# Attention kernel: VectorE's gather, statistics and root in parts over several steps, the transposed maxima copied by VectorE, the projected sum ahead of a pair of maxima

## The chip, the core and the metric

The kernel runs on one core of one Trainium2 chip. A core has a matrix engine (TensorE, PE in the profile, with its weight loads listed apart as PEld), VectorE (DVE), ScalarE (ACT), GpSimd (POOL) and SyncE (SP, which here only issues transfers). Each engine takes its own instructions strictly in the order in which they were written, and waits on semaphores that other engines or transfers raise. The metric is the device time of one execution in microseconds (us); smaller is better. Inputs and outputs are float32.

## What is computed

Two layers are computed twice in alternation, each added to its input. Layer A is a Fourier mixing of normalised rows, layer B is attention with 32 query heads that share one key head and one value head of width 16:

```python
def _layernorm(x, axis=-1, eps=1e-5): ...   # (x - mean) / sqrt(var + eps)
def _A_ref(x, ...):      # x: (1, 2048, 512)
    a = einsum("bsd,ed->bse", x, dft_hid_re); b = einsum("bsd,ed->bse", x, dft_hid_im)
    return einsum("ts,bse->bte", dft_seq_re, a) - einsum("ts,bse->bte", dft_seq_im, b)
def _B_ref(x, wq, wk, wv, wo):   # 32 heads of 16
    q = heads(x @ wq); k = x @ wk; v = x @ wv
    p = softmax(einsum("bhqd,bkd->bhqk", q, k) * 16 ** -0.5)
    return merge(einsum("bhqk,bkd->bhqd", p, v)) @ wo
x = x + _A_ref(_layernorm(x)); x = x + _B_ref(_layernorm(x))
x = x + _A_ref(_layernorm(x)); x = x + _B_ref(_layernorm(x))
```

## The kernel before

The program is one long instruction list, written by Python loops. Nothing reorders it afterwards: the place in the loops at which a call stands is the place of its instructions in each engine's queue. `make_layer` builds one pair of layers A and B, and it is called twice (L = 0 and L = 1). Each pair has two stages.

`phase_a` is the Fourier mixing, and towards its end the queries, keys and values. It also computes some of the maxima of the scores early. At its very end it gathers the maxima of the first half of row tile 0 (`max_neg`), issues twelve further maxima, and after the third of them `max_rows`.

`phase_b` is the attention. The 2048 query rows are 16 row tiles (i), and each row tile has 32 steps (s_): two halves of the heads times 16 blocks of 128 keys. In one step TensorE computes

- the value products of two steps earlier (`pv`, line 787: eight matrix instructions into the bank z),
- four score products (`score`, line 773) into two pairs of banks named x, which ScalarE turns into exponentials with two instructions (line 776),
- about three products for maxima of later row tiles (`max_half`, line 350) into one of three banks named y, which VectorE reduces to one maximum each (line 351).

The bank y is a pool of three, shared by everything else that is small: the output projection `po`, and the transposed maxima. A bank is used again when its reader has finished, so a matrix product into a y bank waits on the VectorE or ScalarE instruction that read the earlier content.

The softmax needs the maximum of each row before its scores. When all maxima of a row tile are there, `max_neg` (at step 27 of the row tile before) reduces the partial maxima to their negative (`nm`, line 366), rounds it into `ms` (372) and takes the rest of the rounding beside it (373). Two steps later `max_rows` transposes `ms` on TensorE into a y bank (379), copies it to SBUF as `mt` (381) and sends it by four transfers into two extra rows of the transposed queries `qT` (386), so that the score product subtracts the maximum by itself.

The output of a row tile is finished during the next row tile by `out_tasks`, a table from step to calls. At step 12 `o_proj` runs twelve projection products (`o_mm`, lines 86 to 88) into the y bank `po`, with two maxima after the sixth and two after the twelfth (`more_max`), and then `o_add` adds `po` to the residual row in SBUF (`bt["x"]`, line 852) and stores it. In L = 0, where the result is the input of the next layer A, its normalisation follows: `o_stats` at step 14 (statistics by lines 135 and 136), `o_rstd` at step 16 (the inverse root: lines 157, 165 and 166 on VectorE, then three rounds of four small instructions on GpSimd), and the rest on GpSimd at steps 25 to 27. In L = 1 (`last`) these three do nothing. For the last two row tiles no maxima are left, so `o_proj` has its pairs of maxima within row tiles 1 to 14 of each layer.

Of the kernel before, what the change touches and what calls it, by code (L numbers as in the profile page):

```python
# [8 lines left out]
F32 = mybir.dt.float32  # L9
F32R = mybir.dt.float32r  # L10
I32 = mybir.dt.int32
AF = mybir.ActivationFunctionType
ALU = mybir.AluOpType
# [4 lines left out]
P = 128  # L18
# [5 lines left out]
NK = D // P  # L24
TB = 4
NPAIR = H // 2
EPS = 1e-5
# [15 lines left out]
HALF = NPAIR // 2  # L43
# [3 lines left out]
def fnet_mqa_kernel(ctx: ExitStack, tc: tile.TileContext, x_in, ct, dt_, wq, wkv, wo, out):  # L47
# [105 lines left out]
    def ln_rstd(t0, n, table=True, between=lambda: None):  # L153
        v = sb.tile([P, 4], F32, name="lnv", bufs=2)[:, :n]
        w = sb.tile([P, 4], F32, name="lnw", bufs=2)[:, :n]
        r = rs[:, t0:t0 + n]
        nc.vector.tensor_scalar(v, mv[:, t0:t0 + n, 1], EPS, None, op0=ALU.add)
        if table:
            nc.scalar.activation(w, v, AF.Sqrt)
            between()  # L160
            nc.vector.reciprocal(r, w)
            between()
            rounds = 1
        else:
            nc.vector.tensor_scalar(w.bitcast(I32), v.bitcast(I32), 1, None, op0=ALU.logical_shift_right)
            nc.vector.tensor_scalar(r.bitcast(I32), w.bitcast(I32), -1, 0x5F3759DF, op0=ALU.mult, op1=ALU.add)
            rounds = 3
        e = nc.vector if table else nc.gpsimd
        for _ in range(rounds):
            if n == 1 and table:  # L170
                e.scalar_tensor_tensor(w, r, v, r, op0=ALU.mult, op1=ALU.mult)
            else:
                e.tensor_mul(w, r, r)
                e.tensor_mul(w, w, v)
            between()
            e.tensor_scalar(w, w, -0.5, 1.5, op0=ALU.mult, op1=ALU.add)
            between()
            e.tensor_mul(r, r, w)
            between()

    def ln_apply(dst, x, t, eng=None):
        (eng or nc.vector).tensor_scalar(dst, x, mv[:, t, 0:1], rs[:, t:t + 1], op0=ALU.subtract, op1=ALU.mult)
# [4 lines left out]
    def make_layer(L, src, mid, dst, last):  # L187
# [173 lines left out]
            if k is None:  # L361
                o.loaded.add(i)

        def max_neg(i, p0=0, n=NPAIR, k=4):
            nm = sb.tile([P, NPAIR, 2], F32, name="nm")[:, :n, :]
            nc.vector.tensor_reduce(nm, o.mxp[i][:, p0:p0 + n, :, :k], op=ALU.max, axis=AX.X, negate=True)
            if p0 + n == NPAIR:
                o.mxp.pop(i)
            nmv = nm.rearrange("p a g -> p g a")
            ms = sb.tile([P, 2, 2, NPAIR], F32, name="ms").rearrange("p g r a -> p (g r a)")  # L370
            ms = ms[:, :4 * n].rearrange("p (g r a) -> p g r a", g=2, r=2)
            nc.vector.tensor_copy(ms[:, :, 0, :].bitcast(F32R), nmv)
            nc.vector.tensor_sub(ms[:, :, 1, :].bitcast(F32R), nmv, ms[:, :, 0, :])
            st["ms"] = ms

        def max_rows(i, p0=0, n=NPAIR, queue=None):
            queue = queue or nc.sync
            pt = bank("y")[:4 * n, :P]
            nc.tensor.transpose(pt, st["ms"].rearrange("p a b c -> p (a b c)"), ident)
            mt = sb.tile([64, P], F32R, name="mt")[:4 * n, :]  # L380
            nc.scalar.copy(mt, pt)  # L381
            for g in range(2):
                for r in range(2):
                    row = 64 * g + M0 + r
                    q = queue if r else nc.sync
                    q.dma_start(f(o.qT[i][row:row + 1, p0:p0 + n, :]), f(mt[n * (2 * g + r):n * (2 * g + r + 1), :]))
# [148 lines left out]
        def phase_a(extra):  # L535
# [191 lines left out]
            for g in range(4):  # L727
                q_half(14, g, *xt[1], lambda: take(mb, 1 if g else 0))
                if g == 0:
                    v_tr(12, 4, vt[0])  # L730
            max_neg(0, 0, HALF, 5)
            for k in range(12):
                more_max()
                if k == 2:
# [101 lines left out]
        def o_mm(k):  # L836
            if k == 0:
                bt["po"] = bank("y")
            ks = slice(k * P, (k + 1) * P)
            mm3(bt["po"], bt["oh"][:, ks], bt["ol"][:, ks], woh[:, k, :], wol[:, k, :], k == 0, k == NK - 1)  # L840

        def o_proj(i):
            for k in range(NK):
                o_mm(k)
                if k % 2 and i < NT - 1:
                    for _ in range(2):
                        more_max()
                        o.extra += 1
            o_add(i)

        def o_add(i):
            nc.vector.tensor_add(bt["x"], bt["po"], bt["x"])  # L852
# [27 lines left out]

        o.finish = finish

        def o_stats(i):
            if not last:
                ln_stats(bt["x"], i)

        def o_rstd(i):
            if not last:
                ln_rstd(i, 1, table=False)

        def o_ln(i):
            if not last:
# [15 lines left out]
        def phase_b(nxt):  # L908
# [10 lines left out]
            for n in range(NT * NSTEP):  # L919
                i, s_ = divmod(n, NSTEP)  # L920
                if len(behind) == 2:
                    pv(*behind.pop(0))
                behind.append((i, s_))
                g = units[o.done][2] if o.done < len(units) else 1
                for j, m in ((1 - g, 1), (g, 2), (3 - g, 0), (2 + g, 1)):
                    score(i, s_, j)
                    for _ in range(m):
                        if owed(n) >= 1:
                            more_max()
                if i == 0 and 2 <= s_ <= 8 and s_ % 2 == 0:  # L930
                    q_half_store(14, s_ // 2 - 1)
                if n == 12:
                    osp = slot(3, F32R).rearrange("p (a h n) -> p a h n", a=2, h=2)
                if i == 0 and s_ in (12, 14, 16, 18):
                    j = s_ // 2 - 6
                    split_sb(st["wo", j], woh[:, j, :], wol[:, j, :], nc.gpsimd)
                if i > 0:
                    for fn in out_tasks(i - 1).get(s_, ()):
                        fn()
                if s_ == 2:  # L940
                    for j in range(2, NT):
                        if i == max(0, j - 4 if j < 13 else j - 2):
                            qT_load(j)
                for fn in half_tasks(i).get(s_, ()):
                    fn()
                for at, j, p0, np_ in ((NT - AHEAD, i, HALF, HALF), (NSTEP - AHEAD, i + 1, 0, HALF if i == NT - 2 else NPAIR)):
                    if j in (0, NT - 1) or j == i + 1 < NT:
                        if s_ == at:
                            assert done_with(j, p0 + np_ - 1)
                            max_neg(j, p0, np_)  # L950
                        if s_ == at + 2:
                            max_rows(j, p0, np_)
            if nxt is not None:
# [11 lines left out]
        def out_tasks(i):  # L965
            return {
                1: [lambda: o_store(i, 1), lambda: o_sum(i, 1), lambda: x_load(i)], 5: [lambda: o_inv(i, 1)],
                6: [lambda: o_load(i, 1)], 9: [lambda: o_scale(i, 1)], 10: [lambda: o_hi(i, 1)],
                12: [lambda: o_proj(i)], 14: [lambda: o_stats(i)], 16: [lambda: o_rstd(i)],
                25: [lambda: o_ln(i)], 26: [lambda: o_xnh(i)], 27: [lambda: o_xnl(i)],  # L970
            }

# [49 lines left out]
```

## Time and profile before

| quantity | value |
|---|---|
| median of 3 runs | 3721.35 us (3719.64 to 3724.51) |
| the profiled execution | 3724.12 us, its span 3722.3 us |
| busy in the span: PE, DVE, ACT, POOL | 3631.1, 2798.4, 2400.3, 777.3 us |
| phase_b of L = 0 | about 689 to 1866 us of the span |
| phase_b of L = 1 | about 2540 to 3712 us |
| mean granted TensorE clock | 0.990 |

All times inside the execution are us from the start of the span. Where a row has a bracket, such as [0.24 <-PE y L350], the engine sat idle for that long before the row's first instruction, and what ended the wait is named behind the arrow. Rows of the timeline merge neighbouring instructions of one kind (x3 is three of them, and the second number is the time from the first one's start to the last one's end). Consecutive VectorE instructions overlap a little, so three reductions of 0.68 us take 1.89 us. Busy time of PE is modelled from the starts and says little by itself.

### The profile page before, as it was taken

To read this page: it belongs to the slowest core of one execution; us is meant where nothing else is said; L and a number is where in the kernel's file an instruction comes from. 1 tells how busy PE (TensorE), PEld (TensorE's weight loads), DVE (VectorE), ACT (ScalarE), POOL (GpSimd) and SP (SyncE) were. 2 spreads that over 40 slices of the span, in tenths; PEclk is the share of its full clock that TensorE was granted. 3 is DMA by queue.
4 is the path that set the end of the run, shared out by engine and by line. 5 is a ranking of instruction groups with operands and counts; after the bars stand their busy time and mean duration, and the time that the engine had idled before them with its cause. 6 is when DMAs were issued, how large, how long until landed. Compare 5 with 4: busy or idle time off the path is not lost. (4 is left out here: it accounts for less than half of the span.)

```text
span 3722.3 us, 64512 instructions
## 1 busy us (share of the span) xinstructions
PE 3631.1 (98%) x25474; PEld 1909.3 (51%) x25474; DVE 2798.4 (75%) x4767; ACT 2400.3 (64%) x3104; POOL 777.3 (21%) x984
## 2 busy tenths in 40 slices
PE   8999999999999999999999999999999999999999
PEld 6786768533433333334377766684343334333333
DVE  5167978788888888888311779778888888888882
ACT  4322222688888888888933231227888888888888
POOL 5534332111111111111154342421000000000000
PEclk9999999999999999999999999999999999999999
DMA  5444241311111100110143342313111111001100
GB/s 176 133 136 125 97 119 52 101 32 50 33 36 31 49 22 24 33 47 23 40 131 104 129 124 92 110 64 89 47 33 36 33 49 34 22 22 50 33 24 25
DMA packets 204736, 243.00 MB, mean 65 GB/s; under 512 B 36880, under 2 KB 160784, under 8 KB 197264
## 3 DMA queue, kind: packets, MB, share of 16 engines
q1 hardware_dynamic: 199504, 222.08, 20.1%
q0 software_dynamic: 4864, 16.78, 1.5%
q8 instruction: 199, 3.26, 0.4%
q14 instruction: 105, 0.86, 0.1%
q10 hardware_dynamic: 64, 0.02, 0.0%
HBM read 174.58 MB, written 63.17 MB: 64 GB/s over the span
## 5 line engine op out<-in xcount | busy, mean ns | idle before, releaser
L776 ACT ACTIVATE slot<-x 128x1024 f32<-128x1024 f32 x1990 | 1943.1, 1027 | 334.4 <-PE x L773 265.5
L351 DVE TENSOR_REDUCE mxp<-y 128x1 f32<-128x512 f32 x3040 | 1908.1, 684 | 281.5 <-PE y L350 233.3
L787 PE MATMUL z<-slot,v 128*32 128x512 f32 x8192 | 1096.3, 605 | 1.9 <-ACT row L790 1.9
L773 PE MATMUL x<-slot,kz 64*128 64x512 f32 x2956 | 900.9, 447 | 3.6 <-DMA slot<-mt 3.5
L773 PEld LDWEIGHTS x<-slot,kz 64*128 64x128 f32 x2956 | 375.3, 185 | 731.5 <-ACT slot L776 598.5
L350 PE MATMUL y<-kz,slot 64*128 64x512 f32 x2208 | 726.2, 435 | 4.8 <-ACT mt L381 0.7
L338 DVE TENSOR_REDUCE mxe<-y 128x1 f32<-128x512 f32 x832 | 516.4, 682 | 189.4 <-PE y L336 184.7
L660 PE MATMUL x<-ch,xnh 64*128 64x512 f32 (+1 forms) x2048 | 507.8, 390 | 16.3 <-DVE slot L74 8.9
L660 PE MATMUL x<-ch,xnl 64*128 64x512 f32 (+1 forms) x2048 | 475.2, 369 | 0.0
L660 PE MATMUL x<-cl,xnh 64*128 64x512 f32 (+1 forms) x2048 | 474.7, 369 | 0.0
L350 PEld LDWEIGHTS y<-kz,slot 64*128 64x128 f32 x2208 | 349.5, 185 | 94.5 <-DVE mxp L351 27.5
L827 POOL TENSOR_TENSOR row<-row,row 128x256 f32<-128x256 f32 x63 | 46.3, 735 | 1677.8 <-DMA row<-rd 1422.6
L336 PE MATMUL y<-kz,slot 64*128 64x512 f32 (+1 forms) x1088 | 354.3, 420 | 33.7 <-DVE mxe L338 20.7
L78 POOL TENSOR_TENSOR cl<-craw,ch 128x512 fp32r<-128x512 f32 x236 | 303.1, 1303 | 289.2 <-ACT ch L77 229.3
L787 PEld LDWEIGHTS z<-slot,v 128*32 128x32 f32 x8192 | 163.6, 108 | 277.3 <-issue 249.2
L660 PEld LDWEIGHTS x<-ch,xnh 64*128 64x128 f32 x2048 | 268.7, 189 | 69.2 <-issue 16.4
L660 PEld LDWEIGHTS x<-ch,xnl 64*128 64x128 f32 x2048 | 280.7, 189 | 33.3
L660 PEld LDWEIGHTS x<-cl,xnh 64*128 64x128 f32 x2048 | 281.7, 190 | 28.0
L77 ACT CAST ch<-craw 128x512 fp32r<-128x512 f32 x256 | 154.8, 620 | 161.8 <-PE x L660 89.5
L666 ACT COPY junk<-x 128x2 f32<-128x2 f32 x256 | 40.5, 158 | 332.3 <-PE x L660 253.6
L336 PEld LDWEIGHTS y<-kz,slot 64*128 64x128 f32 x1088 | 171.8, 188 | 129.4 <-DVE mxe L338 90.5
L338 DVE TENSOR_REDUCE mxp<-y 128x1 f32<-128x512 f32 (+1 forms) x256 | 144.4, 617 | 24.7 <-PE y L336 21.5
(148 smaller groups left out, 3141.7 us busy)
## 6 DMA issues: line engine op xcount, KB each, us to landing
craw<-ct_in SPq DMA_DIRECT2D x112, 512.0 KB
slot<-qd SPq DMA_DIRECT2D x44, 1024.0 KB
qd<-row SPq DMA_DIRECT2D x144, 128.0 KB
od<-row SPq DMA_DIRECT2D x252, 64.0 KB
row<-x_in SPq DMA_DIRECT2D x32, 256.0 KB
mid<-row POOLq DMA_DIRECT2D x32, 256.0 KB, 2.4
craw<-ct_in SPq DMA_DIRECT2D x32, 256.0 KB
row<-mid SPq DMA_DIRECT2D x32, 256.0 KB
```

The costliest lines, as they stand in the source:

```text
L77: nc.scalar.copy(hi, raw)
L78: (eng or nc.vector).tensor_sub(lo, raw, f(hi))
L336: nc.tensor.matmul(pm[g], o.qT[i][gs, pr, :], kz[gs, c0:c0 + n], start=True, stop=True)
L338: nc.vector.reduce_max(to[:, g:g + 1], pm[g], axis=AX.X)
L350: nc.tensor.matmul(pm, o.qT[i][gs, pr, :], kz[gs, kb * 512:kb * 512 + 512], start=True, stop=True)
L351: nc.vector.reduce_max(partial(i)[:, pr, g, kb:kb + 1], pm, axis=AX.X)
L660: nc.tensor.matmul(z[d][:, cols], w, hl[j][t == 1][rs_], start=m == 0 and ph == 0 and j == t == 0, stop=j == 1 and t == 2 and (ph == 0 or ...
L666: nc.scalar.copy(junk, zp[dd][:, :, cols.start])
L773: nc.tensor.matmul(st["e"][:, g, :], kz[64 * g:64 * g + KR, c * P:(c + 1) * P], o.qT[i][64 * g:64 * g + KR, cp:cp + 4, :], start=True, sto ...
L776: nc.scalar.activation(ptiles[i, s_][:, 2 * w:2 * w + 2, :], st.pop("e"), AF.Exp, scale=DH ** -0.5)
L787: nc.tensor.matmul(a[32 * j:32 * j + 32, :], v1[:, c, :], pt[:, j, :], start=c == 0, stop=c == NT - 1)
L827: nc.gpsimd.tensor_mul(bt["ot"][:, cs], bt["ot"][:, cs], bt["den"][:, cs])
```

## The change

Four edits. First, `max_neg` is cut in two: the negative maximum is reduced at step 27, and `max_split` does the rounding and its rest at step 28; the call at the end of `phase_a` still does both at once (`whole`). Second, the copy of the transposed maxima to `mt` goes from ScalarE to VectorE, at the same place in the program. Third, `o_add` is called right after the twelfth projection product, ahead of the second pair of maxima. Fourth, the statistics of a finished row are taken in two halves of 256 columns at steps 14 and 15, put together at step 16, and the three VectorE instructions of the inverse root come one by one at steps 17, 18 and 19, with GpSimd's part behind the last of them.

```diff
+    def ln_piece(t, k):
+        r = rs[:, t:t + 1]
...
+        if k == 0:
+            nc.vector.tensor_scalar(v, mv[:, t:t + 1, 1], EPS, None, op0=ALU.add)
+        elif k == 1:
+            nc.vector.tensor_scalar(w.bitcast(I32), v.bitcast(I32), 1, None, op0=ALU.logical_shift_right)
+        elif k == 2:
+            nc.vector.tensor_scalar(r.bitcast(I32), w.bitcast(I32), -1, 0x5F3759DF, op0=ALU.mult, op1=ALU.add)
+        else:
+            for _ in range(3):
...              # the same four GpSimd instructions as in ln_rstd
-        def max_neg(i, p0=0, n=NPAIR, k=4):
+        def max_neg(i, p0=0, n=NPAIR, k=4, whole=False):
             nm = sb.tile([P, NPAIR, 2], F32, name="nm")[:, :n, :]
             nc.vector.tensor_reduce(nm, o.mxp[i][:, p0:p0 + n, :, :k], op=ALU.max, axis=AX.X, negate=True)
...
+            st["nm"] = nm
+            if whole:
+                max_split()
+
+        def max_split():
+            nmv = st.pop("nm").rearrange("p a g -> p g a")
...
             nc.vector.tensor_copy(ms[:, :, 0, :].bitcast(F32R), nmv)
...
             mt = sb.tile([64, P], F32R, name="mt")[:4 * n, :]
-            nc.scalar.copy(mt, pt)
+            nc.vector.tensor_copy(mt, pt)
...
-            max_neg(0, 0, HALF, 5)
+            max_neg(0, 0, HALF, 5, True)
...
         def o_proj(i):
             for k in range(NK):
                 o_mm(k)
+                if k == NK - 1:
+                    o_add(i)
                 if k % 2 and i < NT - 1:
                     for _ in range(2):
                         more_max()
                         o.extra += 1
-            o_add(i)
...
-        def o_stats(i):
+        def o_stats(i, h):
             if not last:
-                ln_stats(bt["x"], i)
-
-        def o_rstd(i):
+                if h == 0:
+                    bt["st"] = sb.tile([P, 2, 6], F32, name="bst2")
+                nc.vector.bn_stats(bt["st"][:, h, :], bt["x"][:, 256 * h:256 * h + 256])
+
+        def o_aggr(i):
             if not last:
-                ln_rstd(i, 1, table=False)
+                nc.vector.bn_aggr(mv[:, i, :], bt["st"].rearrange("p a b -> p (a b)"))
+
+        def o_rstd(i, piece):
+            if not last:
+                ln_piece(i, piece)
...
                             max_neg(j, p0, np_)
+                        if s_ == at + 1:
+                            max_split()
                         if s_ == at + 2:
                             max_rows(j, p0, np_)
...
-                12: [lambda: o_proj(i)], 14: [lambda: o_stats(i)], 16: [lambda: o_rstd(i)],
+                12: [lambda: o_proj(i)], 14: [lambda: o_stats(i, 0)], 15: [lambda: o_stats(i, 1)], 16: [lambda: o_aggr(i)],
+                17: [lambda: o_rstd(i, 0)], 18: [lambda: o_rstd(i, 1)], 19: [lambda: o_rstd(i, 2), lambda: o_rstd(i, 3)],
```

VectorE's queue in L = 0 from the middle of one row tile on, before. `mxp<-y` are the maxima of line 351, `row<-y,row` is the sum of `o_add`, and `bst`, `mv`, `lnv`, `lnw`, `rs` are the statistics and the root:

```order
L351 TENSOR_REDUCE mxp_14018<-y 128x1 x25
L852 TENSOR_TENSOR row_14537<-y,row_14537 128x512
L351 TENSOR_REDUCE mxp_14018<-y 128x1 x6
L135 BN_STATS bst<-row_14537 128x6
L136 BN_AGGR mv<-bst 128x2
L351 TENSOR_REDUCE mxp_14018<-y 128x1 x6
L157 TENSOR_SCALAR lnv<-mv 128x1
L165 TENSOR_SCALAR lnw<-lnv 128x1
L166 TENSOR_SCALAR rs<-lnw 128x1
L351 TENSOR_REDUCE mxp_14018<-y 128x1 x17
```

The same place after (line 372 is line 351 of before, 880 is 852):

```order
L372 TENSOR_REDUCE mxp_14024<-y 128x1 x23
L880 TENSOR_TENSOR row_14544<-y,row_14544 128x512
L372 TENSOR_REDUCE mxp_14024<-y 128x1 x8
L915 BN_STATS bst_14872<-row_14544 128x6
L372 TENSOR_REDUCE mxp_14024<-y 128x1 x3
L915 BN_STATS bst_14872<-row_14544 128x6
L372 TENSOR_REDUCE mxp_14024<-y 128x1 x3
L919 BN_AGGR mv<-bst_14872 128x2
L372 TENSOR_REDUCE mxp_14024<-y 128x1 x3
L190 TENSOR_SCALAR lnv<-mv 128x1
L372 TENSOR_REDUCE mxp_14024<-y 128x1 x3
L192 TENSOR_SCALAR lnw<-lnv 128x1
```

The sum has moved ahead of two maxima (25 and 6 have become 23 and 8), and one statistics or root instruction now stands alone behind the three maxima of each step, instead of two or three together.

VectorE's queue around the gather of the maxima at steps 27 to 29, before:

```order
L351 TENSOR_REDUCE mxp_14018<-y 128x1 x15
L366 TENSOR_REDUCE nm<-mxp_11944 128x32
L372 CAST ms<-nm 128x2x16
L373 TENSOR_TENSOR ms<-nm,ms 128x2x16
L351 TENSOR_REDUCE mxp_14018<-y 128x1 x30
```

And after, where 387 is the line 366 of before, and 399 and 400 are 372 and 373:

```order
L372 TENSOR_REDUCE mxp_15075<-y 128x1 x15
L387 TENSOR_REDUCE nm<-mxp_12993 128x32
L372 TENSOR_REDUCE mxp_15075<-y 128x1 x3
L399 CAST ms<-nm 128x2x16
L400 TENSOR_TENSOR ms<-nm,ms 128x2x16
L372 TENSOR_REDUCE mxp_15075<-y 128x1 x3
L408 CAST mt<-y 64x128
L372 TENSOR_REDUCE mxp_15075<-y 128x1 x24
```

Three maxima have come between the gather and the rounding, and the copy to `mt` has joined VectorE's queue behind three more.

VectorE's queue at the end of `phase_a` of L = 0, after; before, sixteen maxima followed line 373 without a copy among them, and the copy stood in ScalarE's queue:

```order
L387 TENSOR_REDUCE nm<-mxp_2801 128x16
L399 CAST ms<-nm 128x2x8
L400 TENSOR_TENSOR ms<-nm,ms 128x2x8
L372 TENSOR_REDUCE mxp_2801<-y 128x1 x3
L408 CAST mt<-y 32x128
L372 TENSOR_REDUCE mxp_2801<-y 128x1 x13
```

The copy now stands behind the third maximum. On TensorE, SyncE and GpSimd the instructions stand in the order in which they stood, except that GpSimd's part of the root comes three steps later.

More of the change, by code (lines that the diff above doesn't have):

```diff
@@ L179, in ln_rstd @@
             between()
+    part = {}
+    def ln_piece(t, k):
+        r = rs[:, t:t + 1]
+        if k == 0:
+            part["v"] = sb.tile([P, 4], F32, name="lnv", bufs=2)[:, :1]
+            part["w"] = sb.tile([P, 4], F32, name="lnw", bufs=2)[:, :1]
+        v, w = part["v"], part["w"]
+        if k == 0:
+            nc.vector.tensor_scalar(v, mv[:, t:t + 1, 1], EPS, None, op0=ALU.add)
[5 more added lines that the diff above has]
+            for _ in range(3):
+                nc.gpsimd.tensor_mul(w, r, r)
+                nc.gpsimd.tensor_mul(w, w, v)
+                nc.gpsimd.tensor_scalar(w, w, -0.5, 1.5, op0=ALU.mult, op1=ALU.add)
+                nc.gpsimd.tensor_mul(r, r, w)
     def ln_apply(dst, x, t, eng=None):
@@ L368, in max_neg @@
                 o.mxp.pop(i)
-            nmv = nm.rearrange("p a g -> p g a")
+            st["nm"] = nm
[3 more added lines that the diff above has]
+            nmv = st.pop("nm").rearrange("p a g -> p g a")
+            n = nmv.shape[2]
             ms = sb.tile([P, 2, 2, NPAIR], F32, name="ms").rearrange("p g r a -> p (g r a)")
```

## The prediction

> **What bounds the kernel now.** I read the table of windows by stage first, then the timeline of one undisturbed step, then those steps of a row tile that are longer than that, and last the list of who waited for the instructions that the change moves. The windows are the two attention stages, the start of the first, and then single steps of row tile 8 of the first attention (the start of one exponential to that of a later one); the columns are PE, PEld, DVE, ACT and POOL busy, the granted PE clock and the transfers.
>
> ```profile
> core 0: us, PE busy (x) PEld busy (x) DVE busy (x) ACT busy (x) POOL busy (x), PEclk, DMA share, GB/s
> 672.00:697.00 25.00, 23.52 (x108) 12.72 (x107) 20.10 (x41) 10.60 (x17) 3.26 (x6) 0.80 0.59 174
> 697.00:1866.00 1169.00, 1158.95 (x7816) 455.99 (x7812) 977.52 (x1671) 1005.84 (x1102) 168.47 (x349) 1.00 0.12 36
> 2548.00:3712.00 1164.00, 1156.60 (x7807) 454.82 (x7805) 962.87 (x1596) 1003.56 (x1099) 64.91 (x108) 1.00 0.12 35
> 1303.26:1305.39 2.13, 2.13 (x18) 0.84 (x17) 1.89 (x4) 1.94 (x3) 0.00 (x0) 1.00 0.00 0
> 1305.39:1311.77 6.38, 6.17 (x31) 3.15 (x30) 4.63 (x8) 1.94 (x2) 0.00 (x0) 1.00 0.01 3
> 1311.77:1314.47 2.70, 2.59 (x19) 1.12 (x18) 2.22 (x5) 2.01 (x2) 0.62 (x1) 1.00 0.27 99
> 1318.72:1325.46 6.74, 6.72 (x48) 2.71 (x48) 6.15 (x13) 6.30 (x7) 3.44 (x13) 1.00 0.20 42
> 3167.16:3173.73 6.57, 6.57 (x48) 2.55 (x47) 5.67 (x10) 6.21 (x8) 0.00 (x0) 1.00 0.20 41
> 1346.73:1349.29 2.56, 2.56 (x19) 1.07 (x19) 1.89 (x4) 2.08 (x4) 0.00 (x0) 1.00 0.02 6
> ```
>
> Attention is 2333 of 3722 us, and there neither DVE (84%) nor ACT (86%) is full. A plain step takes 2.13 us, of which PE is busy all the time, DVE 1.89 and ACT 1.94. In the timeline of such a step both come back to PE at every turn:
>
> ```profile
> 1341.65 0.18 PEld L773 LDWEIGHTS x<-xnh,kz 64*128 64x128 f32 x1 [0.84 <-ACT slot L776]
> 1342.22 1.88 DVE L351 TENSOR_REDUCE mxp<-y 128x1 f32<-128x512 f32 x3 [0.24 <-PE y L350]
> 1342.48 1.94 ACT L776 ACTIVATE slot<-x 128x1024 f32<-128x1024 f32 x2 [0.19 <-PE x L773]
> 1342.78 0.16 PEld L787 LDWEIGHTS z<-slot,v 128*32 128x32 f32 x8 [0.24 <-issue]
> ```
>
> So a step is PE's own sequence, and from its first score load to its value products it takes 1342.78 - 1341.65 = 1.13 us. The 0.84 us beside the first row is PEld's alone: the value products run then. Work taken from ACT (0.19 idle a step) or DVE (0.24 idle) is worth something only where PE stands still for it. The longer steps show such places: the two windows of step 12 and 13 take 9.08 us where two plain steps and twelve projection products stand, steps 16 to 18 take 0.17 us more in L = 0 than in L = 1 (6.74 against 6.57), and step 29 takes 2.56.
>
> **The sum ahead of the pair of maxima.** The list by line, the waiters of line 852, and the timeline around step 13:
>
> ```profile
> L852 DVE TENSOR_TENSOR row<-y,row 128x512 f32<-128x512 f32 x32 | 21.8, 682 | 53.1 <-PE y L88 53.1
>   PE y L88: 53.1, 4
>   PEld y L350: 11.6, 28
> 1309.21 0.39 PE L88 MATMUL y<-slot,slot 128*128 128x512 f32 x1
> 1309.52 0.49 PE L350 MATMUL y<-kz,slot 64*128 64x512 f32 x2
> 1310.05 1.29 DVE L351 TENSOR_REDUCE mxp<-y 128x1 f32<-128x512 f32 x2 [0.72 <-PE y L350]
> 1310.94 0.18 PEld L773 LDWEIGHTS x<-xnh,kz 64*128 64x128 f32 x1 [0.84 <-issue]
> 1311.26 0.68 DVE L852 TENSOR_TENSOR row<-y,row 128x512 f32<-128x512 f32 x1
> 1311.99 0.18 PEld L350 LDWEIGHTS y<-kz,slot 64*128 64x128 f32 x1 [0.41 <-DVE row L852]
> 1311.99 0.29 PEld L773 LDWEIGHTS x<-xnh,kz 64*128 64x128 f32 x2
> 1312.65 0.16 PEld L787 LDWEIGHTS z<-slot,v 128*32 128x32 f32 x8 [0.36 <-issue]
> ```
>
> Only 4 of 32 sums waited for their product; 28 stood behind the two maxima, and each of those 28 kept a load of line 350 waiting, 11.6 / 28 = 0.41 us. The reader sees why: the product ends at 1309.60, but DVE, idle for 0.72 us, takes the two maxima at 1310.05 and the sum at 1311.26. The third maximum of step 13 needs the bank of `po`, and loads at 1311.99; PE keeps its order, so the scores behind it wait too, and the value products come at 1312.65 where 1310.94 + 1.13 = 1312.07 would be undisturbed.
>
> After the change the sum can start at about 1309.60, plus the 0.04 that DVE needed behind the pair's products (1309.52 + 0.49 = 1310.01 to 1310.05), plus 0.07 estimated for its semaphores: 1309.71. DVE instructions follow each other at 0.61 (two in 1.29, the last 0.68), so the maxima start at 1310.32 and 1310.93 and the second ends at 1311.61. The first maximum of step 13 now takes `po`'s bank, free since 1310.39, the second that of the earlier of the pair, and the third that of the later: it loads at 1311.61 + 0.05 = 1311.66 instead of 1311.99 (the 0.05 is how long the loads came behind DVE's end: 1311.26 + 0.68 = 1311.94 to 1311.99). That is 0.33 to 0.35 us earlier, and all of PE behind it moves with it; some 0.2 remain. I take 0.35, times 28: -9.8 us. Bounds: nothing (the sum starts no earlier than 1310.05) and the whole 1312.65 - 1312.07 = 0.58, -16.2. What queues behind the sum on DVE are the two maxima, 0.27 later; nobody needs them before the third load. The twelve products, PE's and GpSimd's instructions stay.
>
> **Statistics and root in parts.** In L = 1 these instructions don't exist, so the difference of the windows of steps 16 to 18, 0.17 us, is what they cost: DVE falls behind there, and a maximum's bank comes late. In parts, each step carries one. A half of the statistics is not in the trace; 0.34 (half of the row's 0.68) and 0.68 bound it, and it is nearest to the maximum over 256 columns:
>
> ```profile
> L338 DVE TENSOR_REDUCE mxp<-y 128x1 f32<-128x256 f32 x64 | 24.4, 420 | 8.5 <-PE y L336 5.4 <-PE x L660 0.9
> L135 DVE BATCH_NORM_STATS2 bst<-row 128x6 f32<-128x512 f32 x64 | 43.4, 678 | 1.7 <-DMA row<-x_in 1.4
> 1344.02 0.27 DVE L366 TENSOR_REDUCE nm<-mxp 128x32 f32<-128x128 f32 x1
> 1344.33 0.18 DVE L372 CAST ms<-nm 128x32 fp32r<-128x32 f32 x1
> 1344.55 0.19 DVE L373 TENSOR_TENSOR ms<-nm,ms 128x32 fp32r<-128x32 f32 x1
> 1344.66 0.68 DVE L351 TENSOR_REDUCE mxp<-y 128x1 f32<-128x512 f32 x1
> ```
>
> 0.42 it is, of which the next instruction overlaps 0.07 (0.68 against 0.61): 0.35, against the 0.24 idle plus that same 0.07, 0.31. It fits but for 0.04; the smaller pieces fit. -0.17 x 14 row tiles = -2.4 us (bounds: 0, and the same). GpSimd's twelve small instructions start three steps, 6.4 us, later, and are needed at step 25, 12 us further on: nothing.
>
> **The gather in two steps and the copy on DVE.** Before, gather and rounding put 1344.66 - 1344.02 = 0.64 us between two maxima, 0.33 more than 0.31; the next step shows it at PE, then the transposition follows:
>
> ```profile
> 1345.86 2.50 DVE L351 TENSOR_REDUCE mxp<-y 128x1 f32<-128x512 f32 x4
> 1346.59 0.18 PEld L350 LDWEIGHTS y<-kz,slot 64*128 64x128 f32 x1 [0.39 <-DVE mxp L351]
> 1347.24 0.11 PEld L379 LDWEIGHTS y<-ident,ms 128*64 128x64 f32 x1 [0.35 <-DVE mxp L351]
> 1347.46 0.16 PEld L787 LDWEIGHTS z<-slot,v 128*32 128x32 f32 x8
> L381 ACT CAST mt<-y x36: 237/252/255, 682.4 to 3676.6; 64x128 fp32r<-64x128 f32 x28, 32x128 fp32r<-32x128 f32 x8
> ```
>
> In two parts (0.27 less overlap; 0.18 + 0.19 + their gap, 0.33 in all) both nearly fit, and the load at 1346.59 comes in time. But the transposition needs the bank of its step's first maximum, the second of the four in the first row, which runs from 1346.46 to 1347.14 and starts when PE delivers it. It could load at 1347.19 instead of 1347.24, and its own 0.22 us on PE remain. So of the 2.56 us hardly anything goes: -0.02 x 30 places (15 a layer) = -0.6 us; bounds 0 and -(2.56 - 2.13 - 0.22) = -0.21 x 30 = -6.3. ACT's copy of 0.25 is not on PE's path: ACT idles for PE right behind. On DVE the copy is bounded by the cast of 0.18 above and the 256-column maximum of 0.42, and I take 0.28 (128 columns, by the slope from 256 to 512 of 1.0 ns a column). It stands behind the step's third maximum, fits in 0.31, and its bank is wanted two maxima later: nothing. Bound: 0.28 x 30 = +8.4 if no slack were there.
>
> The Trainium skill ("Perfetto Trace Analysis", section "Optimizing Scalar/DVE Operations") speaks against this move: it gives VectorE some 125 ns of access overhead on PSUM and ScalarE some 51, so by it the copy gets 0.074 us dearer, an estimate of +2.2 us over 30 places if each were on the path, and the sum would end at 3711.7. No row here shows a VectorE copy from PSUM.
>
> **The start of attention.** There the copy does move on the path. The timeline at the end of `phase_a`, L = 0, and the end of the same wait in L = 1:
>
> ```profile
> 681.38 9.18 DVE L351 TENSOR_REDUCE mxp<-y 128x1 f32<-128x512 f32 x15 [0.47 <-PE y L350]
> 682.45 0.26 ACT L381 CAST mt<-y 32x128 fp32r<-32x128 f32 x1 [0.63 <-PE y L379]
> 687.69 0.28 PEld L773 LDWEIGHTS x<-slot,kz 64*128 64x128 f32 x1 [0.38 <-DMA slot<-mt]
> 2537.97 0.33 PEld L773 LDWEIGHTS x<-slot,kz 64*128 64x128 f32 x1
> ```
>
> The copy ended at 682.71. Behind three maxima it starts at 681.38 + 3 x 0.61 = 683.21 and ends near 683.45, 0.74 later, and the transfers and the first score with it. In L = 0 the score already waited for the transfer: +0.74. In L = 1 PE came without a wait, so part is covered; I take +0.3. Together +1.0 us (bounds 0 and 1.5). PE's clock of 0.80 in this stretch may stretch it a little.
>
> **Sum.** -9.8 - 2.4 - 0.6 + 1.0 = -11.8 us. The profiled execution took 3724.12 us (span 3722.3) and would take 3712.3; the median, 2.77 lower, gives 3721.35 - 11.8 = 3709.55, forecast 3709.5.
>
> **Rivals.** *The place of the sum is worth nothing.* If DVE wakes so late for the sum that it begins at 1310.05, the three instructions end when they did, and the third load waits for a maximum instead. For it: the same work in the same queue. Against it: 0.72 us idle beforehand. -2.4 - 0.6 + 1.0 = -2.0: 3719.35. Chance 0.13.
> *DVE becomes the bound at steps 27 to 29.* Three additions in three consecutive steps leave no gap, and the copy falls on PE in full: +8.4 instead of -0.6, 3718.5. For it: 0.33 and 0.28 against 0.31. Against: the copy's bank is wanted two maxima later. Chance 0.08. The Trainium skill's rule above points this way.
> *Step 29 loses its wait too.* If the transposition loads when PE reaches it: -6.3 instead of -0.6, 3703.8. Against it: its bank. Chance 0.11.
> *Slower: the sum blocks DVE.* It now stands ahead of two maxima and also waits for the residual row's transfer and an earlier store. If these come late, everything behind stands. Each 0.1 us costs 2.8. It starts at 1309.71 in the sum; at 0.42 later the gain is gone (11.8 / 28), and at 0.8 later the time is 3721.35 - 11.8 + 22.4 = 3732. Against it: no row of line 852 waited for a transfer. Chance 0.04.
>
> **How the numbers follow.** The forecast has 0.64, with 3705 to 3713 as its own range. I hold 0.2%, 7.4 us, for what a measurement of this kernel tells from no change. Faster: forecast and step 29, 0.75. Same: the first two rivals, 0.21. Slower: 0.04. The range reaches from the case of step 29, a little below, to the two cases at 3719: 3702 to 3719.
>
> **What would show it.** Line 880 starting with an idle wait for line 88 in nearly all 32 cases, and no load of line 371 waiting for it; the window of steps 12 and 13 at 8.7 instead of 9.08; steps 16 to 18 alike in both layers; step 29 at 2.5 and more, the transposition still held by a maximum; the copy on DVE at 0.2 to 0.35 us; the first exponential some 0.7 us later after its stage's start in L = 0. I am wrong if the third load of step 13 still waits until its old place, or if steps 27 to 30 grow.

## The result, and the profile after

The changed kernel takes 3701.2 us (median of six, 3696.14 to 3704.99) against 3721.18 of the kernel before in the same series: ratio 0.9942, 95% interval 0.9927 to 0.9958. A second series on one chip gave 3699.84 against 3718.55: 0.9948 (0.9936 to 0.9961). Forecast were 3709.5 us and a range of 3702 to 3719: the direction was right, the gain of about 19 us larger than the 11.8 of the sum, and the time lies just below the range.

The profiled execution of after took 3704.5 us, its span 3702.7. The windows of the same places as before (both attention stages; in row tile 8 steps 12, 13, 16 to 18 of L = 0, 16 to 18 of L = 1, and 29), with the same columns:

```profile
689.00:1854.00 1165.00, 1156.91 (x7839) 457.32 (x7838) 983.62 (x1712) 1005.01 (x1087) 167.81 (x348) 1.00 0.13 38
2528.00:3692.00 1164.00, 1157.38 (x7841) 457.65 (x7841) 972.37 (x1622) 1005.48 (x1088) 64.75 (x108) 1.00 0.13 37
1300.29:1306.65 6.36, 6.16 (x33) 3.11 (x33) 4.99 (x9) 1.94 (x2) 0.62 (x1) 1.00 0.01 3
1306.65:1308.99 2.34, 2.34 (x18) 1.02 (x18) 1.88 (x4) 1.94 (x2) 0.00 (x0) 1.00 0.31 116
1313.26:1319.82 6.56, 6.56 (x48) 2.55 (x47) 5.88 (x13) 6.20 (x7) 0.00 (x0) 1.00 0.20 41
3151.62:3158.19 6.57, 6.57 (x48) 2.56 (x47) 5.67 (x10) 6.21 (x7) 0.00 (x0) 1.00 0.21 42
1341.08:1343.61 2.53, 2.42 (x19) 0.99 (x18) 2.07 (x5) 1.94 (x3) 0.00 (x0) 1.00 0.00 0
```

Steps 12 and 13 take 8.70 instead of 9.08, steps 16 to 18 are alike in both layers, and step 29 is hardly shorter (2.56 before). Who made the loads of the maxima wait, first before (line 350), then after (line 371):

```profile
  DVE mxp L351: 38.1, 116
  DVE row L852: 11.6, 28
  issue: 10.1, 28
  ACT mt L381: 2.4, 6
```

```profile
  DVE mxp L372: 27.6, 76
  issue: 10.0, 28
```

The 28 waits for the sum are gone. At step 13 a wait for a maximum that ends earlier has come in their place (with the sum alone moved, the list has 44.6 us in 121 waits for maxima); that their number falls to 76 comes from the gather and the statistics, which alone leave 87 and 106. Gone too are the six entries for ScalarE's copy `mt`, 2.4 us, which the prediction had not read. The same list for the loads of the scores, before (line 773) and after (line 800), shows a second thing that it had not read:

```profile
  DMA slot<-mt: 5.4, 10
  PE y L766: 3.4, 4
```

```profile
  PE y L793: 1.7, 2
  DMA slot<-mt: 1.1, 1
  DMA xnl<-mt: 0.5, 1
```

Ten scores waited 5.4 us for the transfers of the maxima; after, two wait 1.6 us. These are idle times of the weight loads, and in a plain step too 0.84 us of such a time passes while the value products run: the lists say who waited, not what it cost. The timeline around step 13 of row tile 8, after, shows the sum where the prediction put it:

```profile
1304.40 0.18 PEld L371 LDWEIGHTS y<-kz,slot 64*128 64x128 f32 x2 [0.36 <-DVE mxp L372]
1304.57 0.69 DVE L880 TENSOR_TENSOR row<-y,row 128x512 f32<-128x512 f32 x1 [0.35 <-issue]
1305.18 3.10 DVE L372 TENSOR_REDUCE mxp<-y 128x1 f32<-128x512 f32 x5
1306.51 0.18 PEld L371 LDWEIGHTS y<-kz,slot 64*128 64x128 f32 x1 [0.39 <-DVE mxp L372]
1307.17 0.16 PEld L814 LDWEIGHTS z<-slot,v 128*32 128x32 f32 x8 [0.37 <-issue]
```

The sum starts 0.17 us behind the loads of the pair, where the maxima of the pair used to go first, and the third load of step 13 now waits for a maximum.

**Two ways to measure the rest.** The starts of the exponential instructions give the length of each of the 1024 steps of a traced execution; a plain one is 2.125 us. What a step has above that repeats to about 0.02 us between executions, except where transfers count: step 31 of some row tiles, and row tile 0, which as a whole took from 70.5 to 73.5 us in the traces. Totals scatter more, and they go with the clock outside attention: in the traced execution of before it was 0.98 in the 690 us ahead of the first attention and 1.00 within both, and over its executions the mean ran from 0.989 to 0.996. A least-squares fit over 167 executions of 13 kernels, with one constant for each kernel and one common slope, gives 2.1 us (± 0.2) less for 0.001 more clock; one execution at a clock of 0.768, 4195.11 us, is left out of it and of the ratios. "At equal clock" below means the difference of these constants to the kernel before, with a 95% interval. The change is worth -18.0 ± 1.1 us by it. Off the 3721.18 of before that is 3703.2, inside the forecast range; but the forecast had that end for another reason, step 29 without its wait, so such a hit would have been luck.

### The profile page after: what moved, and what is told of

It reads as the page before. It is cut to its first block, busy times and chain, and to the rows that moved or that the text cites. A ratio compares the mean times of both kernels' runs of the same rounds, so it can differ in the third digit from the quotient of the medians.

```text
span 3702.7 us, 64514 instructions
## 1 busy us (share of the span) xinstructions
PE 3611.1 (98%) x25474; PEld 1905.9 (51%) x25474; DVE 2803.8 (76%) x4819; ACT 2390.8 (65%) x3068; POOL 775.7 (21%) x984
## 5 line engine op out<-in xcount | busy, mean ns | idle before, releaser
L800 PE MATMUL x<-slot,kz 64*128 64x512 f32 x2956 | 890.6, 447 | 2.6 <-DMA slot<-mt 1.1
L371 PE MATMUL y<-kz,slot 64*128 64x512 f32 x2208 | 713.2, 432 | 1.4 <-DVE mxp L372 0.6
```

The source lines that it names most:

```text
L371: nc.tensor.matmul(pm, o.qT[i][gs, pr, :], kz[gs, kb * 512:kb * 512 + 512], start=True, stop=True)
L800: nc.tensor.matmul(st["e"][:, g, :], kz[64 * g:64 * g + KR, c * P:(c + 1) * P], o.qT[i][64 * g:64 * g + KR, cp:cp + 4, :], start=True, sto ...
```

## The experiments

**Each part by itself.** Four kernels, each the kernel before with one of the four edits of the diff shown above. In short:

```
the sum:        if k == NK - 1: o_add(i)   ahead of the pair;  o_add(i) behind the loop removed
the copy:       - nc.scalar.copy(mt, pt)
                + nc.vector.tensor_copy(mt, pt)
the gather:     max_neg at step 27, max_split at step 28
the statistics: o_stats in halves at 14 and 15, o_aggr at 16, o_rstd in pieces at 17 to 19
```

> The kernel before with one edit: the projected sum ahead of the second pair of maxima. Theory (the gain is PE standing still less at single places, and the places add up): step 13 falls by 0.36 us in the 14 middle row tiles of L = 0 and by 0.41 in those of L = 1, as between the two traces, nothing else moves: -10.8 us in all. The prediction's own term was -9.8. Rival (the parts help each other: the sum is worth this much only because the copy and the statistics relieve VectorE too): step 13 stays above 0.3 over the plain step and the gain is under 7 us.

> The kernel before with one edit: the transposed maxima copied by VectorE. Theory (ScalarE's copy was on PE's path only where the second half of the maxima is transposed, step 13 of row tiles 0 and 15): row tile 15 falls by 0.9 us in each layer (steps 13 to 15) and row tile 0 by 0.45 (step 15), -2.7 us; the first exponential of each layer comes later by 0.8 and 0.3: in all -1.6 us; step 29 of the other row tiles stays at 0.44 over a plain step or grows a little, because gather and rounding still stand together. Rival (the gain of row tiles 0 and 15 came from cutting the gather in two): they stay at 65.1 and 73.5 us here, and the time is +1 us.

> The kernel before with one edit: gather and rounding of the maxima in two steps, the copy still by ScalarE. Theory: step 29 falls from 0.44 to 0.41 over a plain step at 30 places, -0.9 us, and row tiles 0 and 15 stay at 73.5 and 65.1 us. Rival (the cut gather gave the gain of row tiles 0 and 15): they fall by 0.45 and 0.9 us in each layer, and the time by 3.6 us.

> The kernel before with one edit: statistics and root in parts at steps 14 to 19. Theory: steps 16 to 18 of L = 0 fall to those of L = 1, 0.17 us in 14 row tiles, -2.4 us, and L = 1, which has no such instructions, stays as it was. Rival (the statistics also held up step 13 and the start of the next row tile): L = 0 gains over 5 us.

What a step has over 2.125 us, median of row tiles 1 to 14 (for row tile 0 its step 15, for row tile 15 its length), both layers where there are two numbers:

| | before | sum | copy | gather | statistics | after |
|---|---|---|---|---|---|---|
| step 13, L0 and L1 | 0.57, 0.57 | 0.21, 0.15 | 0.57, 0.57 | 0.57, 0.57 | 0.57, 0.57 | 0.21, 0.15 |
| steps 16 to 18, L0 | 0.36 | 0.37 | 0.37 | 0.36 | 0.20 | 0.19 |
| step 29 | 0.44 | 0.44 | 0.44 | 0.41 | 0.45 | 0.41 |
| row tile 0, step 15 | 0.25, 0.22 | 0.24, 0.23 | -0.20, -0.20 | 0.23, 0.21 | 0.25, 0.22 | -0.20, -0.20 |
| row tile 15, us | 65.1, 65.0 | 65.1, 65.0 | 64.1, 64.1 | 65.1, 65.0 | 65.1, 65.0 | 64.1, 64.1 |
| median, us (before in the same series 3718.87) | | 3706.47 | 3712.82 | 3719.38 | 3715.66 | |
| ratio, 95% interval | | 0.9965 (0.9952 to 0.9978) | 0.9984 (0.9975 to 0.9994) | 0.9999 (0.9989 to 1.0008) | 0.9992 (0.9982 to 1.0001) | |
| at equal clock, us | | -10.7 ± 1.6 | -4.6 ± 1.1 | -0.7 ± 1.1 | -2.2 ± 1.1 | -18.0 ± 1.1 |

Each edit moves its own row and no other, and each row moves as far alone as together with the others. The four totals add up to -18.2, and the whole change gave -18.0: within some 2.5 us, the intervals of the four together, nothing is left over for the parts to do to each other. All four first theories hold for the places; only the copy's total is larger than its theory said, -4.6 against -1.6.

**The copy taken back.** The kernel after with `nc.scalar.copy(mt, pt)` again.

> The kernel after with one edit undone: ScalarE copies the transposed maxima again, the gather stays cut in two. Theory (the copy on VectorE pays only where the second half of the maxima is transposed): row tile 15 rises from 64.1 to 65.0 us and row tile 0 by 0.45 in each layer, +2.7 us; the first exponentials come 0.7 and 0.1 us earlier; step 29 of the other row tiles stays at 0.41 over a plain step: +1.9 us in all. Rival (the copy is worth 6 us, the middle of what it gave alone): +6 us, and steps other than those grow.

3706.33 us (before 3717.64), ratio 0.9973 (0.9963 to 0.9982), at equal clock -13.2 ± 1.2: the copy is worth 4.8 us here too. The total lies nearer to the rival's, the places are the theory's: row tile 15 is back at 65.1 and 65.0, step 15 of row tile 0 at 0.25 and 0.24, step 29 stays at 0.41. These places make up 2.8 us; where the rest may lie, the lists of waits suggest, first for the scores (line 800), then for the loads of maxima (line 371):

```profile
  DMA slot<-mt: 4.8, 10
  PE y L793: 3.4, 4
  DMA xnl<-mt: 1.1, 1
```

```profile
  DVE mxp L372: 27.0, 76
  issue: 10.0, 28
  ACT mt L408: 2.4, 6
```

The scores wait 5.9 us in 11 places for transfers of the maxima, against 1.6 in two with VectorE's copy. From the start of the transposition to the end of its copy the traces give 1.59 us with ScalarE and 1.33 with VectorE at step 29 (1.56 and 1.30 in the kernels with the gather uncut), and 2.06 against 0.60 at step 13 of row tile 15. ScalarE takes the copy behind an exponential of a microsecond. With VectorE the transfers go out that much earlier, and a few row tiles start with a wait for them. That this makes up the rest of the 4.8 us is not shown.

**Where the copy counts.** Two kernels from before with the copy on VectorE at some places only (`p0` is not zero for the second half of the maxima, at step 13 of row tiles 0 and 15):

```diff
-            nc.scalar.copy(mt, pt)
+            (nc.vector.tensor_copy if p0 else nc.scalar.copy)(mt, pt)   # first kernel: four copies
...
+            (nc.scalar.copy if p0 or queue is not nc.sync else nc.vector.tensor_copy)(mt, pt)   # second: 30 copies
```

> The kernel before with one edit: VectorE copies the transposed maxima only where the second half is transposed (step 13 of row tiles 0 and 15), four copies of 36. Theory (a bank held by ScalarE's late copy keeps PE waiting at these four places and nowhere else): row tile 15 falls by 0.9 to 1.0 us and row tile 0 by 0.45 in each layer, -2.8 us; all other steps and the starts of attention as before. Rival (the copy's whole gain is here): -4.6 us, what the move of all copies gave at equal clock.

> The kernel before with one edit: VectorE copies the transposed maxima at step 29 alone (30 copies), ScalarE at the end of the Fourier stage and at step 13. Theory (from the transposition to the end of its copy it takes 1.56 us with ScalarE and 1.30 with VectorE, so the transfers of the maxima go out 0.25 us earlier, and that counts only where the next row tile waits for them, at step 31 of some row tiles): step 31 loses 0.1 to 0.3 in four or five row tiles, -0.5 to -1 us in all. Rival (nothing waits for these transfers): 0 us. Second rival (ScalarE's relief counts at every step 29): step 29 falls below 0.44 and the time by 3 us or more.

The four copies alone: 3715.46 us (before 3719.30), 0.9987 (0.9978 to 0.9996), at equal clock -2.8 ± 1.1; row tile 15 at 64.1 in both layers and step 15 of row tile 0 at -0.21 and -0.20. The 30 copies alone: 3717.87 us, 0.9998 (0.9989 to 1.0007), -0.5 ± 1.1; step 29 stays at 0.45, so the second rival is out, and step 31 loses 0.1 to 0.3 us in three places, row tile 1 of L = 0 and row tile 14 of both layers, where the theory had four or five (row tiles 0, 8 and 10 vary too much between traces to tell). The total cannot tell this theory from the rival of 0 us.

The theory of the four copies holds for the places and the size, but not for its cause, the held bank. In row tile 0, TensorE does wait for that bank at step 13 (before, at 721.36; the row stands further down), yet step 13 has 0.18 over a plain step with this wait and 0.19 after, without it. What fell is step 15, which ends where the first exponential of the second half starts, and the score of that one waited for the transfers. Before, then after:

```profile
721.33 2.83 SPq L386 DMA_DIRECT2D slot<-mt  x4
725.44 0.47 PE L773 MATMUL x<-slot,kz 64*128 64x512 f32 x1 [0.24 <-DMA slot<-mt]
```

```profile
720.17 2.83 SPq L413 DMA_DIRECT2D slot<-mt  x4
```

After, the transfers start 1.35 us behind the transposition (at 718.82) instead of 1.81 (at 719.52), and no score waits for them. The size of the wait counts too: with the 30 copies alone, in L = 1 of the one traced execution, TensorE stood still there for 0.95 us instead of 0.22 before, and step 15 came to 0.97 instead of 0.22. The timeline of before at step 13 of row tile 15 and what follows shows what the four copies cost:

```profile
1828.51 1.08 ACT L768 ACTIVATE slot<-y 128x512 f32<-128x512 f32 x2
1829.47 0.24 ACT L381 CAST mt<-y 32x128 fp32r<-32x128 f32 x1
1829.62 1.02 ACT L776 ACTIVATE slot<-x 128x1024 f32<-128x1024 f32 x1
1829.65 0.18 PEld L766 LDWEIGHTS y<-slot,kz 64*128 64x128 f32 x1 [0.31 <-ACT slot L768]
1829.74 1.37 SPq L386 DMA_DIRECT2D slot<-mt  x2
1832.72 0.18 PEld L773 LDWEIGHTS x<-slot,kz 64*128 64x128 f32 x1 [0.84 <-PE y L766]
1833.75 0.18 PEld L773 LDWEIGHTS x<-slot,kz 64*128 64x128 f32 x1 [0.84 <-DMA slot<-mt]
```

In this row tile no maxima are left, and half of the scores go through the y banks to ScalarE (line 768): ScalarE works without a pause, the copy of 0.24 lies on its way, and the transfers, at 1829.74, come so late that the second score of the second half waits until 1833.75. After, with the copy at 1818.62 for a transposition at 1818.30, no score waits for a transfer there.

**The 32 others back to ScalarE.** The kernel after with the first of the two lines above, in the same series as after (3699.84):

> The kernel after itself, beside the next two on the same chip. Theory (its gain is 16 to 18 us inside attention, and the rest of a measured difference comes from the two stretches outside, which vary from execution to execution): its two attention stages last 1164 and 1162.5 us again; its median lies 16 to 18 us below that of the kernel before. Rival (20 us or more are really gained, some outside attention): the median lies 20 us or more below.

> The kernel after with one edit: VectorE copies the transposed maxima only where the second half is transposed (step 13 of row tiles 0 and 15, four copies), ScalarE the other 32. Theory (those four copies are all that the move gains, and the start of attention is what it loses): row tile 15 stays at 64.1 us and step 15 of row tile 0 at -0.2, as with all copies on VectorE; step 29 elsewhere stays at 0.41; the first exponentials come 0.8 and 0.1 us earlier: -0.9 us against the kernel after. Rival (the 32 other copies take work from ScalarE that PE would wait for): +2 us or more, with steps 29 and 30 above 0.41 over a plain step.

After again has its 1164.29 and 1162.10 us of attention. Its median is 18.7 below that of before in this series (3718.55), between the two ranges; at equal clock, with the first series, it is 18.0 ± 1.1, the upper end of the theory's. With 32 copies back on ScalarE the places are as the theory said (row tile 15 at 64.1, step 15 of row tile 0 at -0.21 and -0.19, step 29 at 0.41), and the traced attention stages, 1164.70 and 1161.65, sum to the same 2326.4 as those of after. But the median is 3703.54 (0.9958, 0.9945 to 0.9970), -15.0 ± 1.5 at equal clock: 3.0 ± 1.8 slower than after, where the theory had 0.9 faster. No step of the traced execution shows these 3 us. Step 31, at which transfers count, varies from execution to execution, and only one execution is traced; that the others waited longer there would fit, but is not shown. The rival had 2 us or more, but by steps 29 and 30, and these did not grow.

**The bank at step 29.** The kernel after with `max_rows` behind the next step's value products:

```diff
                     pv(*behind.pop(0))
+                for at, j, p0, np_ in (...):        # the tuple of the loop below
+                    if ... and s_ == at + 3:
+                        max_rows(j, p0, np_)
...
-                        if s_ == at + 2:
-                            max_rows(j, p0, np_)
```

> The kernel after with one edit: the transposition of the maxima and all behind it comes after the next step's value products instead of before them (from the end of step 29 to the front of step 30, and from 13 to 14 in row tiles 0 and 15). Theory (at step 29 TensorE waits for the bank of the step's first maximum, which is free 0.84 us later, and only the transposition's own 0.22 us is TensorE work): step 29 falls from 0.41 over a plain step to nothing and step 30 rises to 0.22, -0.19 us at 30 places, -5.7 us. Rival (the 0.41 is the transposition itself and its change of shape on TensorE): the 0.41 only moves to step 30, 0 us.

3699.03 us, 0.9951 (0.9936 to 0.9966), -19.8 ± 1.7 at equal clock. Step 29 has 0.23 instead of 0.41 over a plain step in both layers, and step 30 nothing (the moved transposition still lies between the exponentials of step 29 and those of step 30, so the 0.22 that the theory had at step 30 is counted at step 29): the 0.18 was the wait for the bank, the 0.23 is TensorE's own work, as the theory said. But the gain against after is 1.8 ± 2.0 and not 5.7: row tile 15 grew from 64.1 to 64.7 and 64.5, because its transfers of step 13 now come later, and by the list of waits seven scores wait 4.0 us for such transfers instead of two for 1.6.

**The bank at step 12.** The kernel after with the projection behind the next step's value products and the second pair of maxima one step later still:

```diff
                     pv(*behind.pop(0))
+                if i > 0 and s_ == 13:
+                    o_proj(i - 1)            # without its second pair
+                if i > 0 and s_ == 14:
+                    two_max()                # the pair
```

> The kernel after with one edit: the twelve projection products and the sum come after the next step's value products (front of step 13 instead of end of step 12), and the second pair of maxima after those of step 14. Theory (at step 12 the first projection product waits 0.25 us for the bank of the step's first maximum): steps 12 and 13 together lose 0.25 us in 28 row tiles, -7 us, and the 0.16 to 0.21 that step 13 still has over a plain step moves to step 14, since a pair ahead of three maxima still leaves VectorE behind. Rival (VectorE gets further behind when the pair stands right ahead of a step's maxima): step 14 rises by 0.4 or more and the time is the same or up to 5 us longer.

3730.55 us, 1.0035 (1.0021 to 1.0049), +10.5 ± 1.5 at equal clock, 28.5 more than after: the rival was right, and too kind. The wait itself was there and is gone. In the list for the projection's first products (line 86) after has this row, and this kernel has none like it:

```profile
  DVE mxp L372: 5.8, 28
```

But steps 12 and 13 lose only 0.21 together (in L = 0, 4.48 to 4.27 over two plain steps), although the second pair, some 0.43 us on TensorE (in after, from its loads at 1304.40 to the value products at 1304.83), has left them, and step 14 rises by 1.18. The timeline there:

```profile
1308.17 0.69 DVE L883 TENSOR_TENSOR row<-y,row 128x512 f32<-128x512 f32 x1 [0.36 <-issue]
1308.78 1.87 DVE L372 TENSOR_REDUCE mxp<-y 128x1 f32<-128x512 f32 x3
1308.92 0.18 PEld L371 LDWEIGHTS y<-kz,slot 64*128 64x128 f32 x1 [0.61 <-DVE row L883]
1310.57 0.19 PEld L371 LDWEIGHTS y<-kz,slot 64*128 64x128 f32 x2 [0.84 <-DVE mxp L372]
1311.11 1.89 DVE L372 TENSOR_REDUCE mxp<-y 128x1 f32<-128x512 f32 x3 [0.45 <-PE y L371]
1311.85 0.18 PEld L371 LDWEIGHTS y<-kz,slot 64*128 64x128 f32 x1 [0.75 <-DVE mxp L372]
1312.45 0.18 PEld L371 LDWEIGHTS y<-kz,slot 64*128 64x128 f32 x1 [0.41 <-DVE mxp L372]
```

With three banks and 0.6 us for a maximum, five maxima in a row leave the fourth and fifth (1311.85 and 1312.45) waiting for VectorE, and at step 13 the third waits for the sum, which now stands right ahead of three maxima. Between the pair and the next three, the value products were the pause in which VectorE caught up.

**A version from these.** The kernel after, the transposition of step 29 alone moved, the copy at the end of `phase_a` back on ScalarE:

> The kernel after with two edits: ScalarE copies the transposed maxima at the end of the Fourier stage alone, and only the transposition of step 29 goes behind the next step's value products (that of step 13 in row tiles 0 and 15 stays). Theory (each place keeps what it gave by itself): step 29 falls from 0.41 to 0.23, row tile 15 stays at 64.1 us, the first exponentials come 0.8 and 0.1 us earlier, and the first scores of row tiles whose transfers of maxima are late come up to 0.4 us later: -0.18 x 30 - 0.9 + 1 = -5.3 us against the kernel after. Rival (the transfers of the maxima, now 0.8 us later, hold up the next row tile everywhere): step 31 rises by 0.2 or more in most row tiles and the time is that of the kernel after or longer.

3697.80 us against 3699.84 of after in the same series, 0.9942 (0.9929 to 0.9956), -20.2 ± 1.5 at equal clock. It has the lowest median of all; its lead over after, 2.2 ± 1.8 at equal clock, is smaller than the 5.3 expected. Step 29 is at 0.23, row tile 15 at 64.1; step 31 has 0.04 more in the median row tile, which takes back about 1 us in 28. The traced attention stages are 1162.48 and 1159.10, 4.8 us shorter than those of after.

## Why the prediction was right on three parts and wrong on the copy

- **The sum ahead of the pair, -9.8.** Right. Step 13 fell by 0.36 in L = 0 and by 0.42 in L = 1, where 0.35 was forecast: 14 x 0.36 + 14 x 0.42 = -10.9, and alone it gave -10.7 ± 1.6. "Some 0.2 remain": 0.21 and 0.15 do. The third load waits for a maximum, and the windows of steps 12 and 13 give the 8.7 that was named. Of the 32 sums, 16 started when their product ended by the profile, and 16 show `issue`, so that sign was read too strictly. No row shows the 0.07 that the working adds for semaphores; in the timeline above the sum started 0.09 behind its product's end (1304.48 to 1304.57), where 0.04 and 0.07 were taken.
- **Statistics in parts, -2.4.** Right: steps 16 to 18 went from 0.36 to 0.19, 14 x 0.17 = 2.4, and alone it gave -2.2 ± 1.1. Half of the statistics took 0.416 us by the list of lines; 0.42 was estimated.
- **The gather, -0.6.** Right: step 29 lost 0.03 at 30 places, 0.9, and the bank holds the transposition, as the run that moved it showed.
- **The start of attention, +1.0.** Right in sign, and about half. The copy starts 3.09 us behind the gather's start instead of 2.35, the 0.74 forecast, and in L = 0 of this trace the first score's load comes 0.79 later behind the gather (8.39 instead of 7.60), in L = 1 only 0.08 (7.17 instead of 7.09). It varies, too. From the gather to the first exponential, L = 0 took 9.63 to 9.68 us in three traces with VectorE's copy there and 8.85 in two, against 8.77 to 9.19, 8.97 in the mean of nine, with ScalarE's; L = 1 took 8.85 against 8.78. That is +0.4 and +0.1.
- **The copy: the step that failed.** The prediction said "ACT's copy of 0.25 is not on PE's path: ACT idles for PE right behind", and read that from one step 29. It holds there. It does not hold at step 13 of row tiles 0 and 15: the prediction left out that the copy stands behind exponentials in ScalarE's queue, that the transfers start only behind it, and that the scores of the second half need them, and in row tile 15 that ScalarE is full. Worth +1.0 in the sum (its start), the copy measured -4.6 ± 1.1. The four copies of step 13 are -2.8 of it, the 30 of step 29 about -0.5, the start +0.5; the 1.8 that these leave is about as large as the intervals of the fit and was not placed. Who waited for ScalarE's copies (line 381) stands in the profile of before:

```profile
  PEld y L350: 1.7, 4
  PE y L350: 0.7, 2
```

The prediction quoted the row of these copies, 0.25 us each, and not these two of who waited. TensorE did, in six entries: with the four copies of step 13 on VectorE, four entries (1.8 us) stay, those of the two starts. The other two are at step 13 of row tile 0; the one of L = 0 before:

```profile
721.07 0.24 ACT L381 CAST mt<-y 32x128 fp32r<-32x128 f32 x1
721.36 0.18 PEld L350 LDWEIGHTS y<-kz,slot 64*128 64x128 f32 x1 [0.33 <-ACT mt L381]
```

These two did not lengthen their step, as said above; what cost time there was the wait for the transfers behind the copy. Such waits stand in the list of the scores, 5.4 us in ten entries, and these were the entries to read. The copy on VectorE itself lasts 0.27 us, where 0.28 was taken:

```profile
L408 DVE CAST mt<-y x36: 269/273/279, 682.2 to 3656.4; 64x128 fp32r<-64x128 f32 x28, 32x128 fp32r<-32x128 f32 x8
```

The Trainium skill ("Perfetto Trace Analysis", section "Optimizing Scalar/DVE Operations") gives VectorE some 0.125 us of access overhead on PSUM and ScalarE some 0.051, by which a copy would be 0.074 us dearer on VectorE, an estimate. Here the copy took 0.273 against 0.252, 0.02 more, and what counted was when it ended: its engine's queue, not its access.

**The rivals.** The place of the sum did count, VectorE did not become the bound at steps 27 to 29 (27 and 28 are at 0.00), step 29 kept its wait, and the sum blocked nothing. The low end of the range came from one of them, step 29 without its wait; that the copy could gain anything was in no case.

## What to carry to other kernels

When an operation moves from one engine to another, look up who waited for it over the whole program, and for the transfer behind it, by place and not at one typical step: the first and last tiles, in which other engines are full, can hold the whole effect. Where a chain of engines is bound by one, lengths of steps show single places to a few hundredths of a microsecond and add up, while totals scatter by several. An instruction that frees a bank goes ahead of others that nobody needs soon, but a burst of such instructions needs a pause behind it: where the value products between two groups of maxima were taken away, that step grew by 1.18 us, and the kernel with this and the later projection took 28 us more.

## What the runs showed of the hardware

Times differed with the mean granted clock by more than several of these edits are worth: 2.1 us for 0.001, with 0.989 to 0.996 for one and the same kernel. It is the stretches outside attention that vary: from the start of the span to the first exponential the traces gave 684.1 to 690.5 us, though the edits change at most 1 us there, while an attention stage of after repeated within 0.4 us (1163.92 and 1164.29, 1162.44 and 1162.10).
